# First loads of a sliding-window attention kernel: the first query tile in four transfers, the first keys ahead of the limits' words, and one cast less

## The chip, the cores and the metric

The kernel runs on one core of a Trainium2 chip. The metric is the device time of one execution in microseconds (us); before the change it is 372.97 us, the median of three runs (372.47 to 373.00).

## The reference

Three stages follow each other, in float32: attention with sink tokens and a window, a gated feed-forward part with a convolution of three taps along the sequence, and four causal attention experts of which each token takes two. Only the start of the first stage is touched. Cut to what matters:

```python
B, H, S, D = 2, 8, 768, 64           # batch, heads, sequence, head size; n_sink = 4, window = 128
scores = np.matmul(q, k.transpose(0, 1, 3, 2)) / np.sqrt(D)
rel = pos[:, None] - pos[None, :]
keep = (pos[None, :] < n_sink) | ((rel >= 0) & (rel < window))
a = softmax(np.where(keep, scores, -1e9))
x = a @ v                            # [B, S, H * D]
h = relu(x @ w_in);  g = sigmoid(conv3(h));  x = (h * g) @ w_out
# then, for four experts e: out += w_e * softmax(causal(q_e k_e^T / 8)) v_e wo_e, two of four per token
```

`n_sink` and `window` are inputs, so the masks are made on the chip from them.

## The kernel before

The sequence is cut into six tiles of 128 rows, the eight heads into four pairs. A step of the first stage is one query tile and one pair: 24 steps for each of the two batches. `a1_S` multiplies a query tile with its one or two key tiles on TensorE (line 484), VectorE adds the mask and takes the row's minimum of the negated scores (line 486, the result `nm`), ScalarE takes the exponential (line 489), TensorE transposes it (line 545), ScalarE copies the transposed tile out of PSUM (line 501), and TensorE multiplies it with the values (line 587). The weights of the feed-forward part arrive as float64 words in `raw` tiles; they are turned into float32 pairs between the steps of attention, by ScalarE (line 339) and VectorE (lines 343, 346, 349). The convolution's weights `cw` take the same path.

A query tile in SBUF holds two blocks for each pair: head 0 in partitions 0 to 63 of block j = 0, head 1 in partitions 64 to 127 of block j = 1, and zeros elsewhere. So line 484 for j = 0 needs the transfer of the upper rows, for j = 1 that of the lower rows. The key tile 0 comes in two transfers, pairs 0 and 1 first (line 263).

`words` are the 16 bytes of `n_sink` and `window`, sent to all 128 partitions in one transfer (line 1171). `limits` turns them into float32 (lines 166 to 171), `masks` makes the mask `m0` of query tile 0 from them (lines 211 and 212; `m` in the trace).

The order of the instructions is written out by hand: each engine, and each of the two engines that issue transfers (SyncE, whose queue is SP, and ScalarE), takes its own instructions in that order. A transfer that waits to be issued holds all that stands behind it on its engine; on ScalarE that includes the exponentials. There are eight semaphores for the landing of transfers, DMAHW0 to DMAHW7, handed out in turn over the transfers of both queues: the ninth transfer waits, before it is issued, until the first has landed, and so on. In the program before the first eight are, in this turn: first query tile j = 0, words, keys 0 (pairs 0 and 1), first query tile j = 1, keys 0 (pairs 2 and 3), keys 1, values 0, second query tile j = 0.

TensorE first multiplies zeros 18 times (line 238).

Of the kernel before, what the change touches and what calls it, by code (L numbers as in the profile page):

```python
# [15 lines left out]
ALU = mybir.AluOpType  # L16
# [3 lines left out]
B, H, S, D = 2, 8, 768, 64  # L20
P = 128
NT = S // P
NPAIR = H // 2
# [65 lines left out]
class Kernel:  # L89
# [72 lines left out]
    def limits(self):  # L162

        nc = self.nc
        wf, neg = self.sm(4, "wf"), self.sm(4, "neg")
        nc.vector.tensor_copy(wf, self.words)
        nc.vector.tensor_scalar(neg, wf, 0.0, 4294967296.0, op0=ALU.is_lt, op1=ALU.mult)
        nc.vector.tensor_tensor(neg, neg, wf, op=ALU.add)
        wf2 = wf.rearrange("p (a two) -> p a two", two=2)
        neg2 = neg.rearrange("p (a two) -> p a two", two=2)  # L170
        nc.vector.scalar_tensor_tensor(self.lims[:, :, None], wf2[:, :, 1:2], 4294967296.0, neg2[:, :, 0:1],
                                       op0=ALU.mult, op1=ALU.add)
# [76 lines left out]
    def load_qkv(self, b, n, lo, hi):  # L249

        t = self.qkv.setdefault(b, {})
        src = getattr(self, n)[b]
        if n == "k" and b:
            t[n, lo] = self.Wt([P, NPAIR, KW], s="k")
            self.nc.sync.dma_start(t[n, lo], src[:, lo])
            return
        if n == "k":
            if lo == 0:
                t["k"] = self.Kt([P, NT, NPAIR, KW])

            for c in (range(0, NPAIR, 2) if lo == 0 else (None,)):
                pr = slice(None) if c is None else slice(c, c + 2)
                self.nc.sync.dma_start(t["k"][:, lo:hi, pr], src[:, lo:hi, pr])
            return
        for tt in range(lo, hi):
            if n == "q":
                if b:

                    half = self.qbuf[tt // 2 % 2].rearrange("p a j c -> p (a j c)")[:, tt % 2 * DM : (tt % 2 + 1) * DM]
                    t[n, tt] = half.rearrange("p (a c) -> p a c", c=P)  # L270
                    self.nc.sync.dma_start(t[n, tt], src[:, tt].rearrange("p (a c) -> p a c", c=P))
                    continue
                t[n, tt] = self.qbuf[tt % 2]
                for j in range(2):
                    rows = slice(j * D, (j + 1) * D)
                    (self.nc.scalar if tt < 2 else self.nc.sync).dma_start(
                        t[n, tt][rows, :, j, :], src[rows, tt].rearrange("p (a c) -> p a c", c=P))
                continue
            t[n, tt] = self.Wt([P, DM], s=n)
            self.nc.sync.dma_start(t[n, tt], src[:, tt])  # L280
# [842 lines left out]
    def program(self, general):  # L1123
        tc, nc = self.tc, self.nc
# [4 lines left out]
        with ExitStack() as ctx:  # L1129
# [28 lines left out]
            if general:  # L1158
                for f in self.first_loads:
                    f()  # L1160
                for w in (self.win, self.wout):
                    for f in range(NF):
                        self.need(w, f)
            else:
                self.warm()

                self.qbuf = [self.Rt([P, NPAIR, 2, P], F32, "q") for _ in range(2)]
                for i, q in enumerate(self.qbuf):
                    (nc.vector if i == 0 else nc.gpsimd).memset(q[:D, :, 1, :], 0.0)
                    (nc.vector if i == 0 else nc.gpsimd).memset(q[D:, :, 0, :], 0.0)  # L1170
                nc.sync.dma_start(self.words, self.lim)
                for n, lo, hi in (("k", 0, 1), ("q", 0, 1), ("k", 1, 2), ("q", 1, 2), ("v", 0, 2), ("bg", 0, 1),
                                  ("k", 2, 4), ("bg", 1, 2), ("v", 2, 3), ("k", 4, 6)):
                    if n == "bg":
                        self.first_loads[lo]()
                    else:
                        self.load_qkv(0, n, lo, hi)
                    if (n, lo) == ("q", 0):
                        nc.scalar.activation(self.sm(1, "e"), self.zeros[:, :1], AF.Exp)
                self.indices()  # L1180
                self.limits()
                self.masks()
                self.fixed()
                first = [self.attn_phase(b, b * NSTEP, LAGS[b], self.attn_misc(b)) for b in range(B)]
                m1 = NSTEP + MLP_START
# [22 lines left out]
            t = m1 + 2 * NSTEP  # L1208
# [10 lines left out]
            else:  # L1219
                a0, a1 = first  # L1220
                src = {"a0": a0, "a1": a1, "m": m, "late": late}
                ph = self.order(ORD1, src)
            qlo = (t, t1 + 60, [(0, lambda i: self.run_qlater())], 1)
            src = {"c0": c0, "c1": c1, "q1": q1, "qlo": qlo, "q0": q0, "in": swap[0], "out": swap[1]}
# [70 lines left out]
```

## Time and profile before

| | |
|---|---|
| median of three runs | 372.97 us |
| the profiled execution's own time | 372.33 us |
| its span in the profile | 370.5 us |
| TensorE busy | 359.5 us (97%) |
| VectorE / ScalarE / GpSimd busy | 272.3 / 264.3 / 118.5 us |
| moved by transfers | 27.53 MB, of these 0.66 MB issued by ScalarE (q10) |
| granted clock of TensorE | 0.999 |

The median of the runs is 0.64 us above the profiled execution, 1.83 us of whose time lie outside the span. TensorE is busy nearly throughout; its idle time lies in the first 17 us and at the end. In the rows, PE is TensorE's matmul, PEld its weight load, DVE VectorE, ACT ScalarE, POOL GpSimd; SPq and ACTq are the queues that issue transfers. Times are in us from the span's start.

### The profile page before, as it was taken

How to read it: one execution, taken by the hardware profiler on the slowest of the kernel's cores; microseconds unless marked ns; L12 is line 12 of the kernel's file. 1: busy time of each engine (PE TensorE's matmuls, PEld its weight loads, DVE VectorE, ACT ScalarE, POOL GpSimd, SP SyncE). 2: the span in 40 equal slices, each digit the busy share in tenths (PEclk: the TensorE clock that was granted, in tenths of full speed). 3: DMA queues.
4: the chain of work that ended last, by engine and by line, in shares of the span. 5: the costliest groups of instructions: out<-in, count | busy, mean ns of one | idle time of the engine just before them, and what ended most of it. 6: DMA issues, size and time to landing. Idle time of an engine off the chain costs nothing.

```text
span 370.5 us, 8892 instructions
## 1 busy us (share of the span) xinstructions
PE 359.5 (97%) x3166; PEld 331.7 (90%) x3166; DVE 272.3 (73%) x834; ACT 264.3 (71%) x778; POOL 118.5 (32%) x230
## 2 busy tenths in 40 slices
PE   7999999899999999999999999999999999999995
PEld 5687877899899999999999999999999899978984
DVE  5689899999887997878756756139668688578631
ACT  4999998766886766546746866249888698759841
POOL 7014120444432442844421222500034144406310
PEclk9999999999999999999999999999999999999999
DMA  7944765353342300001211010000000000001102
GB/s 181 355 138 131 243 208 181 115 189 125 105 125 70 104 30 31 9 21 29 59 44 44 1 58 3 0 2 0 2 3 1 30 30 28 31 1 58 59 32 93
DMA packets 20404, 27.53 MB, mean 74 GB/s; under 512 B 2080, under 2 KB 12928, under 8 KB 20352
## 3 DMA queue, kind: packets, MB, share of 16 engines
q1 hardware_dynamic: 19120, 26.22, 22.3%
q10 hardware_dynamic: 1232, 0.66, 0.8%
q8 instruction: 27, 0.44, 0.5%
q14 instruction: 25, 0.20, 0.2%
HBM read 23.68 MB, written 3.19 MB: 73 GB/s over the span
## 4 chain that ended last, share of the span: by engine, by line
PE 73%; DVE 14%; ACT 6%; issue 2%; POOL 2%; DMA 1%; ACTq 0%; DVEq 0%
PE psB L797 15%; PE psB L753 14%; PE psB L947 9%; PE psB L1071 5%; PE psB L875 5%; PE psB L1047 4%; PE psB L587 4%; PE psB L1095 3%; PE psB L484 3%; PE psB L545 3%; DVE P L486 3%; PE psB L1010 2%; PE psB L1009 2%; PE psB L471 2%; ACT P L489 2%
## 5 line engine op out<-in xcount | busy, mean ns | idle before, releaser
L797 PE MATMUL psB<-g,wouthf 128*128 128x256 f32 x384 | 70.6, 281 | 0.2 <-POOL g L782 0.2
L797 PEld LDWEIGHTS psB<-g,wouthf 128*128 128x128 f32 x384 | 58.9, 188 | 0.6 <-POOL g L782 0.4
L1035 POOL TENSOR_SCALAR P<-P,r 128x256 f32<-128x256 f32 (+5 forms) x48 | 30.1, 640 | 82.8 <-DVE r L1033 42.1
L753 PE MATMUL psB<-xh,winhf 128*128 128x258 f32 x192 | 56.6, 295 | 0.0
L753 PE MATMUL psB<-xh,winlf 128*128 128x258 f32 x192 | 54.2, 282 | 0.0
L753 PE MATMUL psB<-xl,winhf 128*128 128x258 f32 x192 | 54.2, 282 | 0.0
L797 PE MATMUL psB<-g,woutlf 128*128 128x256 f32 x192 | 53.8, 280 | 0.0
L489 ACT ACTIVATE P<-P,nm 128x260 f32<-128x260 f32 (+2 forms) x96 | 46.4, 485 | 10.1 <-DVE nm L486 9.8
L782 POOL TENSOR_TENSOR g<-ht,g 128x256 fp32r<-128x256 f32 x48 | 33.1, 690 | 52.5 <-ACT g L776 46.9
L769 ACT ACTIVATE ht<-ht 128x256 f32<-128x256 f32 x48 | 20.1, 418 | 28.3 <-DVE ht L767 28.2
L774 DVE SCALAR_TENSOR_TENSOR ht<-ht 128x256 f32<-128x256 f32 x48 | 24.2, 505 | 18.8 <-ACT ht L769 18.8
L753 PEld LDWEIGHTS psB<-xh,winhf 128*128 128x128 f32 x192 | 36.4, 189 | 0.3 <-ACT ht L756 0.2
L753 PEld LDWEIGHTS psB<-xl,winhf 128*128 128x128 f32 x192 | 36.5, 190 | 0.0
L753 PEld LDWEIGHTS psB<-xh,winlf 128*128 128x128 f32 x192 | 36.2, 189 | 0.0
L797 PEld LDWEIGHTS psB<-g,woutlf 128*128 128x128 f32 x192 | 36.2, 189 | 0.0
L760 POOL TENSOR_SCALAR ht<-ht,cw 128x256 f32<-128x256 f32 x24 | 15.0, 626 | 59.8 <-ACT ht L756 52.3
L1020 ACT ACTIVATE P<-P,nm 128x256 f32<-128x256 f32 (+3 forms) x48 | 26.8, 561 | 4.7 <-DVE nm L1014 4.6
L767 DVE SCALAR_TENSOR_TENSOR ht<-ht,cw 128x256 f32<-128x256 f32 x48 | 28.3, 589 | 1.7
L545 PE MATMUL psB<-ident,P 128*128 128x128 f32 x176 | 29.1, 281 | 0.3 <-ACT P L489 0.2
L947 PE MATMUL psB<-yh,wqh 128*128 128x256 f32 x96 | 27.2, 283 | 0.0
L947 PE MATMUL psB<-yl,wqh 128*128 128x256 f32 x96 | 27.0, 281 | 0.0
L947 PE MATMUL psB<-yh,wql 128*128 128x256 f32 x96 | 26.9, 280 | 0.0
(176 smaller groups left out, 975.8 us busy)
## 6 DMA issues: line engine op xcount, KB each, us to landing
raw<-in_w_in_dram SPq DMA_DIRECT2D x8, 512.0 KB, 4.2
raw<-in_w_out_dram SPq DMA_DIRECT2D x8, 512.0 KB, 3.3
v<-in_v_dram SPq DMA_DIRECT2D x12, 256.0 KB, 4.2
R<-rD SPq DMA_DIRECT2D x24, 128.0 KB, 3.0
out_dram<-ot SPq DMA_DIRECT2D x11, 256.0 KB, 2.0
k<-in_k_dram SPq DMA_DIRECT2D x7, 260.0 KB, 3.9
raw<-in_wqkv_dram SPq DMA_DIRECT2D x8, 193.0 KB, 3.3
q<-in_q_dram SPq DMA_DIRECT2D x6, 256.0 KB, 3.6
```

The source lines that it names most:

```text
L489: nc.scalar.activation(Pt[:, j, :N], Pt[:, j, :N], AF.Exp, bias=nmx[:, j : j + 1], scale=-1.0, accum_out=sums[:, j : j + 1])
L545: nc.tensor.transpose(ps[:, j, c, :], Pt[:, j, c0 : c0 + P], self.ident)
L753: nc.tensor.matmul(ps[:, :XW], w[:, f, kc, :], x[:, kc, :], start=(i == 0), stop=(i == len(ops) - 1))
L767: nc.vector.scalar_tensor_tensor(t1, h[:, 2 : 2 + CH], self.cw[:, 2 * NF + f : 2 * NF + f + 1], t1, op0=ALU.mult, op1=ALU.add)
L769: nc.scalar.activation(t1, t1, AF.Tanh)
L774: nc.vector.scalar_tensor_tensor(t1, t1, 1.0, h[:, 1 : 1 + CH], op0=ALU.add, op1=ALU.mult)
L782: eng.tensor_tensor(g[:, 1], t1, g[:, 0].bitcast(F32), op=ALU.subtract)
L797: nc.tensor.matmul(self.m1y[d // 2][:, d % 2, :], w[:, f, d, :], g[:, k], start=(first and i == 0 and d % 2 == 0), stop=(last and i == 2), ...
L875: nc.tensor.matmul(ps[:, :NVG], y[:, kc, ts_], w[:, kc, c0 : c0 + NVG], start=(i == 0), stop=(i == len(ops) - 1))
L947: nc.tensor.matmul(ps, w[:, kc, c0 : c0 + P], y[:, kc, :], start=(i == 0), stop=(i == len(ops) - 1))
L1020: nc.scalar.activation(Pt[:, lo:hi], src, AF.Exp, bias=nm[:, 0:1], scale=sg, accum_out=sums[:, j, i : i + 1])
L1035: nc.gpsimd.tensor_scalar(Ps[j][:, :N], Ps[j][:, :N], r[:, j : j + 1], 1.0, op0=ALU.mult, op1=ALU.mult)
```

## The change

The first query tile (tile 0 of batch 0) is loaded in four transfers in place of two: pairs 0 and 1 of both j, then pairs 2 and 3 of both j. The transfer of `words` moves from the head of SyncE's queue to behind the first half of key tile 0. `limits` reads the int32 words directly; the cast to `wf` is left out.

```diff
@@ limits
-        wf, neg = self.sm(4, "wf"), self.sm(4, "neg")
-        nc.vector.tensor_copy(wf, self.words)
-        nc.vector.tensor_scalar(neg, wf, 0.0, 4294967296.0, op0=ALU.is_lt, op1=ALU.mult)
-        nc.vector.tensor_tensor(neg, neg, wf, op=ALU.add)
-        wf2 = wf.rearrange("p (a two) -> p a two", two=2)
+        neg = self.sm(4, "neg")
+        nc.vector.tensor_scalar(neg, self.words, 0.0, 4294967296.0, op0=ALU.is_lt, op1=ALU.mult)
+        nc.vector.tensor_tensor(neg, neg, self.words, op=ALU.add)
+        wf2 = self.words.rearrange("p (a two) -> p a two", two=2)
@@ load_qkv
                 self.nc.sync.dma_start(t["k"][:, lo:hi, pr], src[:, lo:hi, pr])
+                if c == 0:
+                    self.nc.sync.dma_start(self.words, self.lim)
...
-                for j in range(2):
-                    rows = slice(j * D, (j + 1) * D)
-                    (self.nc.scalar if tt < 2 else self.nc.sync).dma_start(
-                        t[n, tt][rows, :, j, :], src[rows, tt].rearrange("p (a c) -> p a c", c=P))
+                n0 = NPAIR // 2 if tt == 0 else NPAIR
+                for a in range(0, NPAIR, n0):
+                    for j in range(2):
+                        rows = slice(j * D, (j + 1) * D)
+                        (self.nc.scalar if tt < 2 else self.nc.sync).dma_start(
+                            t[n, tt][rows, a : a + n0, j, :], src[rows, tt].rearrange("p (a c) -> p a c", c=P)[:, a : a + n0])
@@ program
-                nc.sync.dma_start(self.words, self.lim)
```

SyncE's queue from its start, before; `k_128` are the keys, `v_138` and the others the values, `raw` the weights' words, and the brackets name the semaphores that a row waits for:

```order
L1171 DMA words<-in_lim_dram 128x4
L263 DMA k_128<-in_k_dram 128x260 x2
L263 DMA k_128<-in_k_dram 128x520
L280 DMA v_138<-in_v_dram 128x512
L280 DMA v_140<-in_v_dram 128x512 [waits DMAHW0_49]
L424 DMA cwraw_99<-in_conv_w_dram 128x24 [waits DMAHW2_49]
L263 DMA k_128<-in_k_dram 128x1040 [waits DMAHW3_49]
L372 DMA raw_144<-in_w_in_dram 128x512 [waits DMAHW4_49]
L372 DMA raw_146<-in_w_in_dram 128x512 [waits DMAHW5_49]
```

The same stretch of SyncE's queue now:

```order
L262 DMA k_127<-in_k_dram 128x260
L264 DMA words<-in_lim_dram 128x4
L262 DMA k_127<-in_k_dram 128x260
L262 DMA k_127<-in_k_dram 128x520
L283 DMA v_140<-in_v_dram 128x512 [waits DMAHW0_49]
L283 DMA v_142<-in_v_dram 128x512 [waits DMAHW1_49]
L427 DMA cwraw_99<-in_conv_w_dram 128x24 [waits DMAHW3_49]
L262 DMA k_127<-in_k_dram 128x1040 [waits DMAHW5_49]
L375 DMA raw_146<-in_w_in_dram 128x512 [waits DMAHW6_49]
L375 DMA raw_148<-in_w_in_dram 128x512 [waits DMAHW7_49]
```

The words stand one place further back, and the first values now wait for DMAHW0. The eight semaphores now belong, in turn, to: first query tile, pairs 0 and 1, j = 0; keys 0 (pairs 0 and 1); first query tile, pairs 0 and 1, j = 1; words; first query tile, pairs 2 and 3, j = 0; keys 0 (pairs 2 and 3); first query tile, pairs 2 and 3, j = 1; keys 1.

ScalarE from its start, before; `q_121` is the first query tile, `q_122` the second, `P` with its numbers the first two steps' scores, the rows in between the loading of the exponential's table:

```order
L276 DMA q_121<-in_q_dram 64x4x128 x2
L1179 ACT_TABLE_LOAD
L1179 ACTIVATE e_133<-zeros_100 128x1 [waits DVE_49]
L276 DMA q_122<-in_q_dram 64x4x128
L276 DMA q_122<-in_q_dram 64x4x128 [waits DMAHW1_49]
L489 ACTIVATE P_180,su_182<-P_180,nm_181 128x128 [waits DVE_49] x2
```

The same stretch of ScalarE now:

```order
L279 DMA q_121<-in_q_dram 64x2x128 x4
L1181 ACT_TABLE_LOAD
L1181 ACTIVATE e_135<-zeros_100 128x1 [waits DVE_49]
L279 DMA q_122<-in_q_dram 64x4x128 [waits DMAHW2_49]
L279 DMA q_122<-in_q_dram 64x4x128 [waits DMAHW4_49]
L492 ACTIVATE P_180,su_182<-P_180,nm_181 128x128 [waits DVE_49] x2
```

The order of the operations is the same, but both transfers of the second query tile now wait for pieces of the first one to land (j = 1 of pairs 0 and 1, j = 0 of pairs 2 and 3), and the first exponential stands behind them.

## Rows read from the trace of the kernel before

**Rows 1.** Windows by stage: us, then busy time (and instructions) of each engine, TensorE's clock, DMA share, GB/s.
```profile
17.00:29.00 12.00, 12.00 (x100) 9.52 (x101) 9.64 (x35) 11.54 (x37) 2.42 (x8) 1.00 0.54 158
...
60.00:200.00 140.00, 138.25 (x1270) 131.19 (x1269) 114.89 (x273) 93.06 (x265) 55.94 (x102) 1.00 0.25 77
200.00:360.00 160.00, 158.93 (x1380) 151.88 (x1380) 107.74 (x369) 116.83 (x330) 46.35 (x74) 1.00 0.06 21
```

**Rows 2.** Timeline of TensorE and its weight load: start, us, engine, line, operation, count, [wait<-releaser].
```profile
1.05 3.82 PE L238 MATMUL psB<-zeros 128*128 128x256 bf16 x18 [1.05 <-DVE zeros L232]
...
5.60 0.94 PE L484 MATMUL psB<-k,q 128*128 128x128 f32 x3 [0.73 <-DMA k<-in_k_dram]
...
17.40 0.30 PEld L484 LDWEIGHTS psB<-k,q 128*128 128x128 f32 x2 [0.19 <-DMA q<-in_q_dram]
```

**Rows 3.** Timeline of VectorE, 3.5 to 7 us.
```profile
3.57 0.17 DVE L166 CAST wf<-words 128x4 f32<-128x4 int32 x1 [0.65 <-DMA words<-in_lim_dram]
...
4.80 0.35 DVE L212 SCALAR_TENSOR_TENSOR m<-kix,lims,pen 128x128 f32<-128x128 int32 x1
6.10 0.29 DVE L486 CUSTOM_DVE_ANT_0 P<-psB,m 128x128 f32<-128x128 f32 x1 [0.95 <-PE psB L484]
...
6.69 0.29 DVE L486 CUSTOM_DVE_ANT_0 P<-psB,m 128x128 f32<-128x128 f32 x1 [0.29 <-PE psB L484]
```

**Rows 4.** Timeline of ScalarE, 5 to 15 us.
```profile
6.43 0.40 ACT L489 ACTIVATE P<-P,nm 128x128 f32<-128x128 f32 x1 [2.75 <-DVE nm L486]
...
7.02 0.40 ACT L489 ACTIVATE P<-P,nm 128x128 f32<-128x128 f32 x1
...
12.50 0.35 ACT L501 COPY PT<-psB 128x256 f32<-128x256 f32 x1
12.92 0.68 ACT L339 ACTIVATE f64u<-raw 128x512 f32<-128x512 f32 x1
```

**Rows 5.** Transfers issued between 6.5 and 7 us: KB each, us from issue to landing.
```profile
raw<-in_w_in_dram SPq DMA_DIRECT2D x1, 512.0 KB, 6.3
```

**Rows 6.** Windows of the first 17 us, columns as in the first group.
```profile
2.00:2.50 0.50, 0.50 (x4) 0.33 (x3) 0.40 (x2) 0.32 (x1) 0.50 (x3) 1.00 0.82 19
2.50:3.00 0.50, 0.50 (x5) 0.36 (x3) 0.39 (x2) 0.50 (x1) 0.42 (x3) 1.00 0.25 10
3.00:3.50 0.50, 0.50 (x4) 0.38 (x3) 0.00 (x0) 0.49 (x2) 0.50 (x2) 1.00 0.55 110
3.50:5.00 1.50, 1.37 (x8) 0.78 (x6) 1.16 (x6) 0.18 (x1) 0.95 (x4) 1.00 1.17 255
...
9.00:13.00 4.00, 3.69 (x25) 2.45 (x24) 2.44 (x17) 3.31 (x16) 0.00 (x0) 1.00 1.04 403
13.00:17.40 4.40, 4.23 (x30) 3.10 (x28) 2.78 (x12) 4.40 (x16) 0.00 (x0) 1.00 1.07 349
```

**Rows 7.** Timeline of SyncE's queue, issues one by one.
```profile
0.73 0.39 SPq L1171 DMA_DIRECT2D words<-in_lim_dram  x1
...
1.18 0.41 SPq L263 DMA_DIRECT2D k<-in_k_dram  x1
...
5.10 0.33 SPq L280 DMA_DIRECT2D v<-in_v_dram  x1
...
6.13 0.33 SPq L263 DMA_DIRECT2D k<-in_k_dram  x1
...
6.62 0.33 SPq L372 DMA_DIRECT2D raw<-in_w_in_dram  x1
```

**Rows 8.** Timeline of ScalarE and its queue, 0.7 to 4.2 us.
```profile
0.73 0.75 ACTq L276 DMA_DIRECT2D q<-in_q_dram  x1
...
1.51 0.64 ACTq L276 DMA_DIRECT2D q<-in_q_dram  x1
2.19 1.28 ACT L1179 ACT_TABLE_LOAD   x1 [2.19 <-issue]
...
3.57 0.60 ACTq L276 DMA_DIRECT2D q<-in_q_dram  x1
```

## The prediction, as it was made before the changed kernel ran

> **What bounds the kernel now.** I read the windows by stage first, then the chain at the start back to what it waits for. From 17 us on TensorE is busy for 12.00 of 12.00 us, then for 138.25 of 140 and 158.93 of 160 [rows 1]. The change touches nothing there, so it can only move the moment at which that stretch begins, and every instruction behind takes over this shift. So the question is what sets the time at 17 us.
>
> Read backwards, the reader is to see three things. At 17.40 a weight load waits 0.19 us for a transfer of a query tile [rows 2]. From 13.0 to 17.4 ScalarE is full, 4.40 of 4.40 us [rows 6]: whatever starts it at 13 sets all that follows. What starts it is line 339, which reads the first block of weight words. ScalarE is free at 12.50 + 0.35 = 12.85 and starts line 339 at 12.92 [rows 4]; this block was issued at 6.62 and landed 6.3 us later, at 12.92 [rows 5, 7]. So the work of attention and the landing of the weights arrive within 0.07 us of each other. Of the two, the later one holds the kernel, and a gain in only one of them is worth 0.07 us.
>
> The transfers are one stream: from 3.5 us on the DMA share is above 1 in each window, at 255 GB/s first and 403 later, while 2.0 to 3.5 us moves hardly anything: 19, 10 and 110 GB/s [rows 6]. All of this is in front of the weight words in the queues.
>
> At the start of attention, the words land at 3.57 and the mask is done at 4.80 + 0.35 = 5.15. The first reduction of line 486 starts at 6.10 only, the second at 6.69, each waiting for TensorE [rows 3]. TensorE itself waited for the keys until 5.60 [rows 2]. The lower half of the query tile landed at 6.13: this is when the key transfer that waits for its semaphore is issued [rows 7]. The exponentials start at 6.43 and 7.02, the second late by the gap between the reductions [rows 4].
>
> **The change part by part.**
>
> The cast goes: 0.17 us of VectorE on the way from words to mask [rows 3]. The next instruction now reads int32; line 212 reads int32 as well and takes 0.35 us for 128 columns, for four columns I take no difference.
>
> The words move back: their issue goes from 0.73 to behind the keys' 0.41 us, where the keys stood at 1.18, so 0.45 later [rows 7]. If they land 0.45 later, that is 4.02. If they also wait for the bytes of the key transfer (130 KB at 255 GB/s, 0.52 us [rows 6]) it is 4.54. I take 4.1, nearer to the first, because the keys get a head start in a stretch that moves nothing else. The mask then needs 1.58 - 0.17 = 1.41 us more: 5.5, between 5.4 and 5.95. That is later than before (5.15) and still ahead of the 6.10 at which it is used now.
>
> The query tile in four pieces: each has half the rows of the two of before. An issue took 0.75 and 0.64 us on ScalarE [rows 8], and 0.39 to 0.41 us for the two shorter ones of SyncE [rows 7]; so four take 1.6 to 3.0 us, and ScalarE comes to the table load (1.28 us) at 2.4 to 3.7 in place of 2.19. That is hidden: nothing on ScalarE is due before 6.43. Pairs 0 and 1 together are the 128 KB that j = 0 alone was; this landed at 5.10 (the issue of values that waited for it [rows 7]). So both j of the first step are there by 5.1 where the second was there at 6.13. With the zeros ended at 1.05 + 3.82 = 4.87 [rows 2], TensorE can start at 5.1, and the reductions at 5.6 and 5.95, led by the mask.
>
> The waits that are added: both transfers of the second query tile now wait on ScalarE, the last one for pairs 2 and 3, j = 0, that is for 192 of the tile's 256 KB. Between 5.10 (128 KB) and 6.13 (256 KB) this is 5.6. The issue takes 0.60 [rows 8], so ScalarE is free for the exponential at 6.2 at the earliest if the pieces come no faster than before. Queued behind it are all exponentials, and behind these TensorE's transposes. So the first exponential is at 6.2 to 6.3 (5.6 + 0.33 = 5.93 if the pieces come sooner), the second follows at once, at 6.65 in place of 7.02. The chain of attention gains 0.4 us, 0.9 at most (start at 4.87), and less than nothing only as in the third rival. The first values wait as well, for a piece that lands at 5.1 or before; they were issued behind 2 us of other transfers, and in a stream that is never empty an issue that is still ahead of its turn costs nothing.
>
> The stream: the bytes ahead of the weight words are the same. What changes is the start. 2.0 to 3.5 us moves 9.5 + 5 + 55 = 70 KB where 255 GB/s would move 382: a hole of 1.23 us. If the key tile is moved in this hole in place of the words, the stream gains 130 KB, 0.52 us. If the words then make a hole of their own, it loses up to 1.23 again. So the shift of the landing at 12.92 lies between 0.52 sooner and 0.71 later. The nearest thing to the words in a full stream is the convolution's transfer (24 words of 8 bytes for a partition), which stands in the queue between the values issued at 5.10 and the keys issued at 6.13, so ahead of the weight words; no window shown between 3.5 and 13 falls below 255 GB/s [rows 6, 7]. So I take a fifth of the hole, 0.25, and a gain of 0.27.
>
> The sum: attention gains 0.4, the stream 0.27; the smaller one counts, and the 0.07 that ScalarE is early is no help, since the landing is the later of the two. The kernel gains 0.27, say 0.3: the profiled execution's 372.33 becomes 372.0. The median of the runs stands 0.64 above it, so the median 372.97 becomes 372.7. A measurement of this kernel tells about 0.2%, 0.75 us, from no change: forecast is no change that can be measured.
>
> **The rivals.**
>
> *The hole belongs to the words alone.* If the slow stretch comes from their being first, and other transfers run at full speed from 2 us on, the stream gains more than attention can use (up to 1.23), and the chain's 0.9 us count: reductions from 5.37 (4.87 and the 0.50 between 5.60 and 6.10), exponentials from 5.7 and 6.1 in place of 7.02. That gives 372.1. For it: 2.0 to 2.5 us shows a DMA share of 0.82 at 19 GB/s, that is, engines busy with next to nothing [rows 6]. Against it: the first query transfer was issued at 0.73 as well and did not run either, which looks like a start that is slow for all.
>
> *The words make the hole again, slower.* They are taken when everything else is queued behind them; the whole 1.23 us is paid, the keys' 0.52 is got back, and the weight words land 0.71 later, at 13.63. ScalarE, full from there, hands this on: 373.7. It decides from the point at which the words hold the stream for over 0.52 us. For it: the share of 0.82 again. Against it: the convolution's small transfer, which costs nothing visible among others. The Trainium skill's page "DMA: Bandwidth & Descriptors", section "Specifications", says that below 512 bytes a piece a transfer falls short of the line rate because of a read-modify-write. By that rule the price would belong to the words wherever they stand; the words' window agrees, the convolution's transfer does not.
>
> *Half the size does not land sooner.* Then pieces need the 4.4 to 4.6 us from issue to landing that the halves of 128 KB took (0.73 to 5.10, 1.51 to 6.13 [rows 7, 8]). The third piece, issued at 1.55 to 2.2, lands at 6.15 to 6.8, the last issue of the second query tile holds ScalarE until 6.75 to 7.4, and the second exponential is at 7.2 to 7.8. That is 0.15 to 0.8 later, of which 0.07 is slack: 373.1 to 373.7. It decides where the third piece lands after 6.1. For it: the two landings 1.03 us apart follow issues 0.78 apart. Against it: they come out of a full stream, where half the bytes are half the time. The same page's section "Rules for kernel authors" advises one transfer over two to disjoint halves of the partitions, since they share the same engines, and its section "Bandwidth" calls transfers under 64 KB bound by their descriptors; the pieces here have 64 KB.
>
> **How the numbers follow.** Forecast 0.56, the hole gone 0.22, the hole again 0.12, no sooner landing 0.10. Under the forecast the shift lies between 0.6 sooner and nothing. The range reaches to the first rival with 0.2 us for the spread of the runs, and nearly to the second: 371.9 to 373.6. Faster by over 0.2% means below 372.22: the first rival and 0.02 of the forecast, 0.24. Slower means above 373.72: most of the second rival's upper end and a part of the third, 0.11. The rest, 0.65, is no change.
>
> **What would show it.** In the profile after: the first reduction at 5.4 to 5.95 with VectorE waiting for the words and not for TensorE; no gap between the first two exponentials, the first at 5.9 to 6.3; the second query tile's issues on ScalarE after 5 us; line 339 on the first weight words 0.2 to 0.3 us before 12.92, and all of TensorE's stages shifted by the same. The step that can fail is the stream: if the first 0.5 us windows from 1.5 us show over 200 GB/s, the first rival holds; if they show a second window below 50 GB/s after 3.5 us, the second. If line 339 starts over 0.3 us before 12.92 and the time does not follow, then I have the wrong gate, and the transfer awaited at 17.40 is the next to look at.

## The result, and the profile after

The changed kernel takes 376.24 us (median of 6 runs, 374.87 to 376.83); the kernel before, on the same chip, 372.95 us (6 runs, 372.44 to 373.05). The ratio is 1.009 with an interval of 1.0077 to 1.0102: 3.3 us slower, where no measurable change was predicted, and outside the predicted range of 371.9 to 373.6. The profiled execution of after took 374.87 us with a span of 373.1, against 372.33 and 370.5 of before. It is the quickest of its runs, so the profile shows 2.5 us of the 3.3. Line numbers behind the change are 2 or 3 higher (484 is now 487, 486 is 489, 489 is 492, 339 is 342), those of the mask 1 lower (212 is now 211).

Windows of after, columns as in [rows 1], answering to [rows 1, 6]:

```profile
2.00:2.50 0.50, 0.50 (x4) 0.33 (x3) 0.40 (x2) 0.00 (x0) 0.50 (x3) 1.00 0.74 230
2.50:3.00 0.50, 0.50 (x5) 0.36 (x3) 0.40 (x2) 0.00 (x0) 0.42 (x3) 1.00 0.46 97
3.00:3.50 0.50, 0.50 (x4) 0.38 (x3) 0.00 (x0) 0.01 (x1) 0.50 (x2) 1.00 0.56 84
3.50:5.00 1.50, 1.50 (x13) 1.28 (x12) 0.78 (x4) 1.47 (x2) 0.63 (x4) 1.00 1.00 313
...
9.00:17.00 8.00, 5.92 (x30) 4.10 (x31) 3.46 (x18) 4.75 (x20) 0.16 (x1) 0.79 1.01 315
17.00:29.00 12.00, 12.00 (x106) 9.57 (x104) 9.74 (x36) 11.46 (x37) 0.98 (x5) 1.00 0.47 133
...
200.00:360.00 160.00, 158.97 (x1383) 152.40 (x1383) 109.25 (x372) 116.40 (x329) 46.53 (x74) 1.00 0.06 20
```

The same window of before:

```profile
9.00:17.00 8.00, 7.52 (x52) 5.34 (x50) 5.22 (x28) 7.31 (x29) 0.00 (x0) 1.00 1.06 374
```

From 17 us on TensorE is as full as before, so the loss lies in front of it: in 9 to 17 us TensorE is busy for 5.92 us and its granted clock is 0.79. Before, it was busy for 7.52 us at 1.00. (The trace has no clock record ahead of the clock's first rise, and the windows show 1.00 there; a rise is read from the records.) Matching the ScalarE instructions of the two traces one by one shows when the shift comes: after is 0.66 us ahead up to 10.5 us, 1.73 behind at 12.4, 2.07 at 14, and 2.2 to 2.5 behind from 17 us to the end.

The start went as intended. VectorE in after, answering to [rows 3]:

```profile
4.12 0.17 DVE L166 TENSOR_SCALAR neg<-words 128x4 f32<-128x4 int32 x1 [1.19 <-DMA words<-in_lim_dram]
...
5.13 0.35 DVE L211 SCALAR_TENSOR_TENSOR m<-kix,lims,pen 128x128 f32<-128x128 int32 x1
5.64 0.29 DVE L489 CUSTOM_DVE_ANT_0 P<-psB,m 128x128 f32<-128x128 f32 x1 [0.15 <-PE psB L487]
...
5.86 0.29 DVE L489 CUSTOM_DVE_ANT_0 P<-psB,m 128x128 f32<-128x128 f32 x1
...
12.52 0.43 DVE L489 CUSTOM_DVE_ANT_0 P<-psB,m 128x256 f32<-128x256 f32 x1 [2.08 <-PE psB L487]
```

The first two reductions start 0.46 and 0.83 us sooner. The last row is the first reduction of the second query tile: VectorE waits 2.08 us for TensorE.

ScalarE and its queue in after, answering to [rows 4, 8]:

```profile
4.62 0.62 ACTq L279 DMA_DIRECT2D q<-in_q_dram  x1
...
5.27 0.63 ACTq L279 DMA_DIRECT2D q<-in_q_dram  x1
5.97 0.40 ACT L492 ACTIVATE P<-P,nm 128x128 f32<-128x128 f32 x1 [0.99 <-DVE nm L489]
...
6.37 0.39 ACT L492 ACTIVATE P<-P,nm 128x128 f32<-128x128 f32 x1
...
9.91 0.22 ACT L342 ACTIVATE f64u<-cwraw 128x24 f32<-128x24 f32 x1
...
12.98 0.51 ACT L492 ACTIVATE P<-P,nm 128x256 f32<-128x256 f32 x1 [2.76 <-DVE nm L489]
...
14.95 0.67 ACT L342 ACTIVATE f64u<-raw 128x512 f32<-128x512 f32 x1
```

The second query tile is issued at 4.62 and 5.27; before, at 2.25 and 3.57. ScalarE is ahead until 10 us, then waits 2.76 us, and reads the weight words at 14.95 where it read them at 12.92 [rows 4]. By the trace's completion records (the semaphore steps that tell of a landing) the words had landed at 12.65 (before: 12.89). So they are not what it waited for.

TensorE in after, 8 to 14 us, and the second query tile's products in before (a product in float32 is two matmul instructions in the trace, so `x4` are the two products of one step):

```profile
8.39 0.71 PE L548 MATMUL psB<-ident,P 128*128 128x128 f32 x2
11.18 2.04 PE L487 MATMUL psB<-k,q 128*128 128x256 f32 x4 [2.08 <-DVE f64u L346]
13.15 1.12 PE L590 MATMUL psB<-PT,v 128*64 128x128 f32 x8
```

```profile
9.59 1.04 PE L484 MATMUL psB<-k,q 128*128 128x256 f32 x4
```

The products of the second query tile wait 2.08 us. The VectorE instruction named as releaser (line 346, started at 10.26) had long ended. What came last is the first half of the query tile, landed at 11.09 by the completion records, the second at 11.36; before, 7.51 and 9.54. After this wait the step's two products take 2.04 us where they took 1.04 before. Windows of after and of before over that stretch:

```profile
11.00:14.00 3.00, 2.82 (x12) 1.90 (x12) 1.14 (x6) 0.88 (x3) 0.00 (x0) 0.50 1.02 402
```

```profile
11.00:14.00 3.00, 2.75 (x20) 1.99 (x15) 2.46 (x15) 2.43 (x9) 0.00 (x0) 1.00 1.03 406
```

Behind its wait TensorE has the lower of its two levels, 1.2 GHz, for the whole 3 us (by the records from 10.79 to 14.20), and gets 12 matmul instructions done in place of 20. So two terms make the loss in this trace: a transfer that lands late, and the clock that falls in the wait for it. The other five executions are 0.7 to 2.0 us longer, and their granted clock over the whole span is 0.988 to 0.992, where the profiled one has 0.995.

### The profile page after: what moved, and what is told of

It reads as the page before. It is cut to its first block, busy times and chain, and to the rows that moved or that the text cites. A ratio compares the mean times of both kernels' runs of the same rounds, so it can differ in the third digit from the quotient of the medians.

```text
span 373.1 us, 8894 instructions
## 1 busy us (share of the span) xinstructions
PE 360.3 (97%) x3166; PEld 332.5 (89%) x3166; DVE 272.5 (73%) x833; ACT 264.7 (71%) x778; POOL 119.0 (32%) x230
## 4 chain that ended last, share of the span: by engine, by line
PE 75%; DVE 13%; ACT 6%; issue 2%; POOL 2%; ACTq 0%; DVEq 0%
PE psB L800 15%; PE psB L756 14%; PE psB L950 9%; PE psB L1074 5%; PE psB L878 5%; PE psB L487 4%; PE psB L1050 4%; PE psB L590 4%; PE psB L1098 3%; PE psB L548 3%; DVE P L489 2%; PE psB L1013 2%; ACT P L492 2%; PE psB L1012 2%; PE psB L474 2%
## 5 line engine op out<-in xcount | busy, mean ns | idle before, releaser
L492 ACT ACTIVATE P<-P,nm 128x260 f32<-128x260 f32 (+2 forms) x96 | 46.4, 485 | 10.8 <-DVE nm L489 10.5
```

What stands on the lines that cost most here:

```text
L492: nc.scalar.activation(Pt[:, j, :N], Pt[:, j, :N], AF.Exp, bias=nmx[:, j : j + 1], scale=-1.0, accum_out=sums[:, j : j + 1])
```

## The experiments

My theory (A): the second query tile, issued late behind four smaller transfers, lands late, and TensorE's wait for it costs the time, in part by the clock. The rivals were that the words or the stream do it (B), and, about the clock, that it costs nothing beside the wait (D).

**1. The first query tile in two transfers again**, all else as in after.

```diff
-                n0 = NPAIR // 2 if tt == 0 else NPAIR
+                n0 = NPAIR
```

> The changed kernel, but with the first query tile in two transfers again; the words stay behind the keys and the cast stays out. Theory A (the two transfers that are added push both transfers of the second query tile behind a landing, they land late, TensorE stands still for them): the first transfer of the second tile waits for nothing again, TensorE has no wait over 0.3 us before line 487 of query tile 1, time 372.4 to 372.8, that is 0 to 0.5 us below the kernel before. Rival B (the words behind the keys, or a stream disturbed by them, make the loss): 375 to 377 as the changed kernel.

Measured: 373.21 us (12 runs), ratio 1.0015 (1.0003 to 1.0028). Most of the loss is gone; the second tile lands at 6.57 and 9.16. So the split makes the loss, as in theory A, and B falls as its main cause: words and keys are here as in after. But nothing is gained: about 0.6 us of loss are left, and the time is 0.4 us above the range that I gave. Its profiled execution took 373.52 us; TensorE in it:

```profile
4.86 0.63 PE L487 MATMUL psB<-k,q 128*128 128x128 f32 x2
6.18 1.65 PE L487 MATMUL psB<-k,q 128*128 128x128 f32 x6 [0.68 <-DMA q<-in_q_dram]
```

The first products start 0.74 us sooner than before, then the lower half of the query tile is awaited until 6.18, as before. And the matmul instructions of the products come 0.21 us apart up to 9.4 us, where before they came 0.11 apart: the trace's clock records show the rise to 2.4 GHz at 10.12 us here, at 4.54 before. That costs this execution 0.9 us.

**2. The split alone**, in the kernel before (words first, cast kept).

```diff
-                for j in range(2):
+                n0 = NPAIR // 2 if tt == 0 else NPAIR
+                for a in range(0, NPAIR, n0):
+                    for j in range(2):
...
```

> The kernel before with the first query tile in four transfers and nothing else. Theory A: 375 to 377, the second query tile lands at 10.5 to 11.5 us and TensorE waits 1.5 to 2.5 us for it. Rival B: 372.5 to 373.5.

Measured: 377.48 us (4 runs), ratio 1.0117 (1.0091 to 1.0142): the split alone does all the harm, and more without the two other edits. ScalarE, TensorE and a window of its profile (of the longest of the four executions, 379.59 us):

```profile
7.68 0.40 ACT L491 ACTIVATE P<-P,nm 128x128 f32<-128x128 f32 x1 [2.70 <-DMA q<-in_q_dram]
```

```profile
8.32 0.62 PE L547 MATMUL psB<-ident,P 128*128 128x128 f32 x2 [1.81 <-POOL m1x L221]
...
12.60 1.19 PE L486 MATMUL psB<-k,q 128*128 128x256 f32 x2 [1.48 <-DVE f64u L345]
```

```profile
9.00:17.00 8.00, 6.36 (x27) 4.14 (x26) 2.90 (x18) 4.32 (x20) 0.00 (x0) 0.53 1.00 319
```

Here the last issue of the second tile (7.03 us) holds ScalarE's first exponential until 7.68, and the tile lands at 12.51 and 13.81; the clock is 0.53 over eight microseconds. By the records it falls at 9.44, in the stretch behind a first wait of 1.81 us: TensorE's transposes need that first exponential, whatever releaser the row names. So the hold of ScalarE, which the prediction's third rival had named, costs here as well, and the run does not show the late tile by itself. The pieces of the first tile land later here than in after (the third at 7.01 against 5.22), which fits the smaller loss in after, where the keys come first.

**3. The second query tile issued by SyncE**, ahead of the values.

```diff
-                        (self.nc.scalar if tt < 2 else self.nc.sync).dma_start(
+                        (self.nc.scalar if tt < 1 else self.nc.sync).dma_start(
```

> The changed kernel with the second query tile's two transfers issued by SyncE, behind the first two key tiles and ahead of the values, in place of ScalarE. Theory A: they land by 7.5 us, ScalarE is never held, the earlier start of the first step is kept up to the landing of the weight words at about 12.65: 372.2 to 372.8. Rival C (the first query tile's four pieces themselves, or what they do to the stream, cost the time): above 374.

Measured: 375.43 us (6 runs), ratio 1.0085 (1.0061 to 1.0109). My number missed, and by the number rival C came (above 374). The tile now lands at 7.39 and 8.33, its products start at 8.96, 0.63 us sooner than before, and the clock holds. ScalarE, TensorE's weight loads and VectorE in its profile show what took over:

```profile
13.42 0.68 ACT L342 ACTIVATE f64u<-raw 128x512 f32<-128x512 f32 x1 [1.21 <-DMA raw<-in_w_in_dram]
```

```profile
18.98 0.30 PEld L487 LDWEIGHTS psB<-k,q 128*128 128x128 f32 x2 [0.43 <-DMA q<-in_q_dram]
```

```profile
25.04 0.69 DVE L532 TENSOR_TENSOR R<-psB,R 128x512 f32<-128x512 f32 x1 [0.96 <-DMA R<-rD]
```

The weight words land at 13.34 in place of 12.89, the third query tile at 18.94 in place of 17.36, and a block of R late as well. Matched against before, ScalarE is 0.64 us ahead up to 12.4, then 0.51, 1.58 and 2.29 behind, one step at each of these waits. So the late second tile makes the loss in after, but bringing it forward in this way isn't enough to be rid of it: the transfers behind it are late. Whether that is due to the four pieces (rival C) or to the two transfers more in SyncE's queue, this run can't tell; run 6 bears on it. Windows of this run and of before at 5 to 6 us:

```profile
5.00:6.00 1.00, 1.00 (x7) 1.00 (x6) 0.69 (x4) 0.07 (x1) 1.00 (x2) 1.00 0.80 205
```

```profile
5.00:6.00 1.00, 0.40 (x2) 0.30 (x2) 0.15 (x1) 0.00 (x0) 1.00 (x2) 1.00 1.16 256
```

The DMA share is 0.80 where it was 1.16: the stream has gaps. SyncE issues each of its transfers only when an earlier one has landed, and here it has two more of them to pass; that this makes the gap is argued, not tried.

**4. Matmuls on zeros in the wait**: after, with 11 dummy products ahead of the second tile's.

```diff
+        if (b, qt, pr) == (0, 1, 0):
+            self.spin(11)
```

> The changed kernel with 11 matmuls of zeros (about 0.2 us each) on TensorE ahead of the first step of query tile 1, in the time in which it waits. They add no work that anything waits for. Theory A with a clock term (TensorE's granted clock falls after the wait, and a part of the loss is work at 1.2 GHz): granted clock 0.997 or more, 373.8 to 374.8; the two products of that step take 1.04 us as before in place of 2.04. Rival D (the lower clock costs nothing, the wait is all): 375.5 to 377, as the changed kernel.

Measured: 374.23 us (8 runs), ratio 1.004 (1.0025 to 1.0056). TensorE and a window of its profile:

```profile
9.05 1.36 PE L237 MATMUL psB<-zeros 128*128 128x256 bf16 x11
10.26 0.60 PE L489 MATMUL psB<-k,q 128*128 128x256 f32 x2
11.98 0.67 PE L489 MATMUL psB<-k,q 128*128 128x256 f32 x2 [1.13 <-DMA q<-in_q_dram]
```

```profile
11.00:14.00 3.00, 2.02 (x15) 1.49 (x16) 1.60 (x9) 1.44 (x6) 0.00 (x0) 1.00 1.03 406
```

The second half of the tile lands even later, at 11.85, yet the step's two products take 0.60 + 0.67 us, not 2.04, the shift stays at 1.23 us to the end, and the granted clock of the whole span is 0.996 to 1.0 in its runs against 0.988 to 0.995 in those of after. With work that computes nothing, 2.0 us of 3.3 are won back, and of the six executions of after the shortest has the highest clock; both speak against rival D. The split of the loss is not clean, since the first half lands at 9.10 here and at 11.09 in after, and the wait that is left is 1.13 us long.

**5. The kernel before once more**, unchanged, for one profile.

> The kernel before, unchanged, for a second trace of it: how much the landings of its first transfers and the moment at which TensorE's clock rises differ from one execution to the next. If they are fixed by the order alone, the first weight words land at 12.9 and the second transfer of the third query tile at 17.4, each within 0.3 us.

Measured: 372.3 us. The landings of the first 17 us are within 0.2 us of the first trace (second half of the second tile 9.51, weight words 12.88, third tile 17.42), but for the first half of the second tile, 7.83 against 7.51; ScalarE is shifted by 0.1 at most. The clock's rise comes at 5.82 us, not 4.54. So in these two executions of one kernel the landings nearly agree and the rise of the clock does not. For the kernels with the split this isn't shown: after and run 4 issue the second tile at the same times, and its first half lands at 11.09 and 9.10.

**6. The second query tile on SyncE, behind the values.**

```diff
-                        (self.nc.scalar if tt < 2 else self.nc.sync).dma_start(
+                        (self.nc.scalar if tt < 1 else self.nc.sync).dma_start(
...
-                for n, lo, hi in (("k", 0, 1), ("q", 0, 1), ("k", 1, 2), ("q", 1, 2), ("v", 0, 2), ("bg", 0, 1),
+                for n, lo, hi in (("k", 0, 1), ("q", 0, 1), ("k", 1, 2), ("v", 0, 2), ("q", 1, 2), ("bg", 0, 1),
```

> The changed kernel with the second query tile issued by SyncE behind the values, so as late as in the changed kernel (4.4 to 5.5 us) but in one queue ahead of the large transfers. If the late issue alone makes it land late: 10.5 to 11.5 us, TensorE waits 1.5 to 2 us for it, 375 to 377. If it lands late because its pieces of 512 bytes share the engines with pieces of 4 KB from the other queue: it lands by 9 us, TensorE waits under 0.3 us for it, and only the later transfers can be late: 373 to 375.5.

Measured: 373.75 us (10 runs), ratio 1.0026 (1.0011 to 1.0042). The two issues are at 4.71 and 5.49, later than in after (4.62 and 5.27), but land 4.4 us later each, at 9.10 and 9.89. In after it takes 6.5 and 6.1 us, in run 4 4.5 and 6.6. So the second of the two expectations came, but for the landing, which is not by 9 us. TensorE waits for the tile for 0.17 us, not 2.08, and of the loss of 3.3 us 0.9 is left. So the late issue alone does not make the loss: it does so together with ScalarE's queue. What the four pieces cost by themselves (rival C of run 3) lies within those 0.9 us, unless something else gained as much. What the two queues moved in after, 5.3 to 9 us, by the view of transfers (q10 holds 512-byte pieces of the query tile and is ScalarE's, q1 is SyncE's; packets, MB, share of 16 engines):

```profile
q1 hardware_dynamic: 543, 1.01, 81.3%
q10 hardware_dynamic: 352, 0.17, 17.3%
```

The same of before, 4.2 to 7.5 us, while the second tile is under way there:

```profile
q1 hardware_dynamic: 410, 0.62, 78.5%
q10 hardware_dynamic: 497, 0.24, 33.9%
```

In after ScalarE's queue gets 0.17 MB in 3.7 us (46 GB/s), in before 0.24 in 3.3 (72 GB/s). The other queue holds values of 2,048 bytes (241 packets) and keys of 4,160 (117) in that stretch of after, and values of 2,048 (103) and keys of 1,040 and 2,080 (268) in before. The Trainium skill's page "DMA: Bandwidth & Descriptors", section "Queues, rings and completion order", says that each DMA engine takes turns between the queues that have work for it, a whole packet of several descriptors at a time. The trace can agree in kind only, since the packets that it counts are single pieces: these, 543 to 352, are nearer to even than the bytes, 1.01 to 0.17 MB. The same page's "Issuing engines are not separate DMA queues" says that issuing from several engines saves only the time of the issue; here the queue, with the values ahead of the tile, was worth 1.7 to 2.1 us of landing against after.

Its profile (of an execution of 375.39 us, one of the longest) also shows the price of putting the tile there, on TensorE and on ScalarE:

```profile
10.03 0.67 PE L487 MATMUL psB<-k,q 128*128 128x256 f32 x2 [0.17 <-DMA q<-in_q_dram]
```

```profile
14.50 0.66 ACT L342 ACTIVATE f64u<-raw 128x512 f32<-128x512 f32 x1 [1.88 <-DMA raw<-in_w_in_dram]
```

**7. Run 3, with SyncE's order changed as well**: the first weight words ahead of keys 2 and 3, keys 4 and 5 behind the third query tile.

```diff
-                                  ("k", 2, 4), ("bg", 1, 2), ("v", 2, 3), ("k", 4, 6)):
+                                  ("bg", 1, 2), ("k", 2, 4), ("v", 2, 3)):
...
+                    if (n, lo) == ("q", 2):
+                        self.load_qkv(0, "k", 4, 6)
```

> The kernel of the third experiment (second query tile on SyncE) with the first weight words ahead of the keys of tiles 2 and 3, and the keys of tiles 4 and 5 behind the third query tile. If what cost that kernel its time are the weight words (13.34) and the third query tile (18.94) landing late in the stream: the first land by 12.2, the second by 18, ScalarE's wait of 1.2 us goes, 372.0 to 373.3. If its cost is elsewhere: 374.5 to 376.

Measured: 374.69 us (6 runs), ratio 1.0058 (1.0039 to 1.0077): in the range that I gave for a cost elsewhere, though the words (12.15) and the third tile (17.63) land as soon as hoped for. ScalarE, TensorE and VectorE in its profile:

```profile
12.24 0.69 ACT L342 ACTIVATE f64u<-raw 128x512 f32<-128x512 f32 x1
```

```profile
17.32 1.12 PE L487 MATMUL psB<-k,q 128*128 128x260 f32 x4 [1.14 <-issue]
```

```profile
24.31 0.69 DVE L532 TENSOR_TENSOR R<-psB,R 128x512 f32<-128x512 f32 x1 [1.49 <-DMA R<-rD]
```

The wait for the weight words is gone and ScalarE is 0.67 us ahead until 16.7. All of that and more is lost between 17 and 26 us, in two steps: TensorE waits 1.14 us until 17.32, just behind the landing of the third tile's first half (17.23), and a block of R (the sums' reciprocals, read back from DRAM) is awaited for 1.49 us. The shift is 1.9 at the end. In runs 3 and 7 other transfers pass their due time when one is brought forward; R's load is issued at 18.68, 0.9 us later than before, and which wait holds it was not tried.

**8. The two moves of order alone**, in the kernel before.

> The kernel before with the same two moves in the order of its transfers. If the landings at 12.92 and 17.40 are what holds the kernel before: the wait of 0.19 us at 17.4 goes and the stages behind begin up to 0.5 us earlier, 372.1 to 372.6. If TensorE's and ScalarE's own work holds it as much: 372.5 to 373.0, no change.

Measured: 372.44 us (12 runs), ratio 0.9994 (0.9983 to 1.0004). Weight words land at 11.51 and the third tile at 16.03, ScalarE reads the words when it comes to them, and the shift is -0.43 to -0.5 from 20 us on. The two rows stand at 12.92 and 18.19 in before:

```profile
12.74 0.69 ACT L339 ACTIVATE f64u<-raw 128x512 f32<-128x512 f32 x1
...
17.97 0.51 ACT L489 ACTIVATE P<-P,nm 128x260 f32<-128x260 f32 x1
```

This is the lowest median of the changed kernels, but no difference that the runs can tell.

**9. Runs 1 and 8 together**: after, unsplit, with the two moves.

> The changed kernel with the first query tile in two transfers again, and with two moves in SyncE's order: first weight words ahead of keys 2-3, keys 4-5 behind the third query tile. Theory A (the loss came from the second query tile's late landing, and what remains is set by the landing of the weight words and the third query tile): weight words read by 11.8 us at the latest, third tile's second half landed by 17.0, a time of 372.1 to 372.9, that is, not above the kernel before. Rival (keys first and words later are themselves late, hidden so far behind the weight words): ScalarE's first exponential later than 6.6 us, that lateness kept to the end, 373.0 to 373.8.

Measured: 373.04 us (10 runs), ratio 1.0011 (1.0001 to 1.0021), 0.1 us above the range of theory A; the rival's late exponential did not come either. ScalarE in its profile (an execution of 372.41 us):

```profile
6.29 0.40 ACT L492 ACTIVATE P<-P,nm 128x128 f32<-128x128 f32 x1 [2.62 <-DVE nm L489]
...
12.66 0.69 ACT L342 ACTIVATE f64u<-raw 128x512 f32<-128x512 f32 x1
```

The weight words land at 10.50, a microsecond sooner than in run 8, but are read at 12.66, not by 11.8 as I expected: ScalarE comes to them only after the attention work, which starts 0.14 us sooner than before [rows 4]. The profile is about 0.5 us ahead of before, the median is not. Part of that can be seen: at the last landing of a transfer the profile is still 0.47 us ahead (368.23 against 368.70), but its span ends at 370.62 against 370.53. What stands behind the last landing took 2.39 us here and 1.83 in before, and 1.64 to 2.39 over all traces of this study, so tenths of a microsecond that are won at the start can be lost there. Beside that, runs 8 and 9 differ by the place of the words and by the cast; their medians lie 0.6 us apart, and if the cast is worth nothing (run 10), the words behind the keys may cost some of it. With intervals that touch, this is not shown.

**10. Run 8 without the cast.**

> The kernel before with the two moves of order (weight words ahead of keys 2-3, keys 4-5 behind the third query tile) and the cast of the limits' words left out, the words still first. Theory A: the cast was never on the path (the first reduction waits for TensorE), so the time is that of the moves alone, 372.2 to 372.6, and the mask is done 0.17 us sooner to no use. Rival (start of attention is the gate once the weight words are early): 0.1 to 0.2 us below the moves alone, 372.0 to 372.3.

Measured: 372.54 us (10 runs), ratio 1.0 (0.9985 to 1.0015): the cast was worth nothing, as a reduction that waits for TensorE says. TensorE and ScalarE in its profile:

```profile
5.59 2.22 PE L483 MATMUL psB<-k,q 128*128 128x128 f32 x8 [0.53 <-DMA k<-in_k_dram]
```

```profile
6.73 0.40 ACT L488 ACTIVATE P<-P,nm 128x128 f32<-128x128 f32 x1 [3.05 <-DVE nm L485]
...
13.66 0.69 ACT L338 ACTIVATE f64u<-raw 128x512 f32<-128x512 f32 x1
```

The eight matmul instructions take 2.22 us; the same eight took 1.49 and 1.47 in the two traces of the kernel before, in which the clock had risen by 4.54 and 5.82 us. Here it rose at 9.94. ScalarE is 0.9 us behind before at 12 us, 0.73 at the weight words (13.66) and 0.55 at 360 us, where run 8, with the same order, is 0.48 ahead. So the late rise is worth about 1.0 us in this trace; the ten executions lie 2.1 us apart.

## Why the prediction was wrong

- **What bounds the kernel.** Right in the main: the first 17 us move, and in after every instruction behind takes over the shift. But I named the landing of the weight words as what sets the time at 17 us, with the third query tile next. The second query tile was missing from that list, and its slack was small: its second half landed at 9.54, and the product that reads it began at 10.04 (the third of the four instructions from 9.59 on).
- **Cast, words, query pieces.** Right in size: words read at 4.12 (4.1 said), mask done at 5.48 (5.5), reductions at 5.64 and 5.86 (5.6 and 5.95), exponentials at 5.97 and 6.37 (6.2 and 6.65). One sign missed: the first reduction still waits for TensorE (0.15 us), not for the words. Run 10 shows no gain from the cast.
- **The stream.** Right at the weight words: 0.24 us sooner (0.27 said). The premise of the sentence on the first values, "in a stream that is never empty an issue that is still ahead of its turn costs nothing", does not hold everywhere: the DMA share is 0.46 and 0.56 from 2.5 to 3.5 us in after, about as in before (0.25 and 0.55), and 0.80 at 5 to 6 us in run 3, where before has 1.16. What the later issue of the values costs in after was not tried.
- **The waits that are added: the step that failed.** I counted the second query tile's two issues only as something that holds ScalarE until 6.2, and asked who waits behind the issue, not who waits for the data. Issued 2.4 and 1.7 us later than before, the halves land 3.6 and 1.8 us later, the first 1.2 us slower in this trace, and TensorE waits 2.08 us. The term for this wait was missing from the sum, in which the chain of attention gains 0.4 us. The issue at 3.57 had taken 6.0 us to land in before; 5.6, the time I gave for the last issue, and 6.0 make 11.6, against a product due at 10.04 less the gain. The numbers for it were there.
- **The clock.** It has no term in the prediction. In the wait of 2.08 us TensorE's clock falls, and it runs at 1.2 GHz from 11 to 14 us. In run 4 that is gone and 2.0 us of 3.3 are won back, with the reservation made there.
- **The rivals.** None of their times came. The hole of [rows 6] shrank (230, 97 and 84 GB/s where 19, 10 and 110 were), so the sign of the first rival, over 200 GB/s, shows in one window only. Half the size did land sooner (the third piece at 5.22), and no second window below 50 GB/s came between 3.5 and 17 us. The rival on the slower side that did come starts from the same two issues as my third one, by their landing, not by ScalarE's time.

What stays open: why the weight words land later in runs 3 and 6 (13.34 and 14.41) than in after (12.65), although the two queues hold the same bytes ahead of them (the trace of run 6 is of one of its longest executions, and its ten lie 3.5 us apart); the gaps in the stream are seen, which of SyncE's waits makes each was not tried.

## What to carry to other kernels

Splitting a transfer into pieces moved the later issues of the same queue here, by 2.4 and 1.7 us; so for each of these follow the data too: issue, duration of the same transfer in the trace, landing, and the instruction that reads it. A gain at the first tile is worth only the slack of the next ones, and a wait on TensorE can cost once more through its clock: behind the 2.08 us here, a step of 1.04 us took 2.04. When a load is made earlier, list the landings that become later, since at the start of this kernel all loads share one stream.

## What was not expected of the hardware

- The same 128 KB in 512-byte pieces took 4.4 us from issue to landing in the queue that also held the values and keys (run 6), and 6.1 to 6.5 in the other queue, beside values of 2,048 and keys of 4,160 bytes (after); in run 4, in that queue, 4.5 and 6.6.
- After a wait of 2.08 us TensorE's granted clock was 0.50 from 11 to 14 us; with 11 dummy products ahead of the same step, and 1.13 us of wait left, it was 1.00.
- The first rise of TensorE's clock, by its records, came at 3.96 us in after, 4.54 and 5.82 in two executions of the same kernel before, 9.94 in run 10 and 10.12 in run 1, while the landings of the two executions of before agreed within 0.2 us, but for one (0.32).
